# Decoding float64 weight words on ScalarE, VectorE and GpSimd: sign by the slope of a parametric Relu, low bits by a pass of ScalarE, one joining pass on VectorE

## The chip, the cores and the metric

One core of a Trainium2 chip. The metric is the device time of one execution in microseconds (us). The kernel before took 958.51 us, the median of 3 runs (957.35 to 958.92).

## What is computed

```python
def reference(q, k, v, w_in, w_out, a, b):        # q, k, v: (8, 8, 576, 64)
    scores = q @ k.T / sqrt(64)                   # causal window of 64 positions
    x = softmax(scores within the window) @ v     # then (B, H, S, D) -> (4608, 512)
    h = x @ w_in                                  # (512, 2048)
    P = a[0] + a[1]*h + a[2]*h**2 + a[3]*h**3
    Q = 1 + abs(b[0])*abs(h) + abs(b[1])*h**2
    return (P / (Q + 1e-6)) @ w_out               # (2048, 512)
```

The two weight matrices arrive as float64. They are handed to the kernel as pairs of 32-bit words, low word first, and the kernel itself makes float32 of them.

## The kernel before

**Tiling.** The 4608 tokens are nine chunks of 512 (`c`). The attention of a chunk is four units `(c, hp)`, one for each pair of heads: scores on TensorE, exponentials on ScalarE, a normalisation on GpSimd (L589), transposes on TensorE, a copy `pT` to SBUF, the product with v (`ps_x`, L608). From `ps_x` come `xh`, a rounded copy, and `xl`, the rest (L613, L617). The feed-forward part goes in steps: step `s` takes one chunk and one 128-wide slice `i` of the 2048 hidden channels. It makes `h` by twelve products of `wi_h`, `wi_l` with `xh`, `xl` (L688), passes `h` through a gate of five ScalarE passes, six VectorE passes and one GpSimd product `u1` (L694 to L733), and adds twelve products of the gate with `wo_h`, `wo_l` into four accumulators (L771). The steps run chunk 0 with slices 0 to 7, then chunk 1 with slices 0 to 15, then chunk 0 with slices 8 to 15, then chunks 2 to 8 with all slices. So the first eight steps, of chunk 0, are steps 0 to 7, and step 8 is the first of chunk 1.

**The decode** (`plan_decode`) makes 32 weight tiles, sixteen of `w_in` and sixteen of `w_out`; tile `n = 2i + z` holds slice `i`. Per tile: a load of 512 KB by SP; `scale` on ScalarE (L393) multiplies the high word, read as float32, by 2^-111 into `w_c`, or into a bank of PSUM from slice 8 on; `sign` on GpSimd (L397) multiplies the high word by zero in place, which leaves its sign bit; `put_sign` on VectorE (L401) shifts `w_c` left by 3 and ors the sign in; `put_low` on VectorE (L406) ors in the top three bits of the low word; `high` on ScalarE (L417) rounds to `wi_h` or `wo_h`; `rest` on VectorE (L420) gives `wi_l` or `wo_l`.

**The order** is made before anything runs by `Plan`. Every operation is added with an engine, a cost, a rank, what it follows and which buffers (`Slot`) it uses. `Plan.order` walks these in a model of time and hands the operations out by their planned start, so every engine's queue is in that order and is never reordered on the chip. Ranks are shifted by tables of numbers (`TILE_AT`, `UNIT_AT`, `GATE_AT`, `OUT_AT`, `FETCH_AT`), and `LI`, `LO` say how many steps before its first use a tile's decode is ranked. `PT_DVE` and `XH_DVE` name the units whose `pT` copy and `xh` copy VectorE makes; ScalarE makes the others.

Of the kernel before, what the change touches and what calls it, by code (L numbers as in the profile page):

```python
# [45 lines left out]
class Plan:  # L46
# [25 lines left out]
    def order(self):  # L72
# [22 lines left out]
        while len(done) < len(self.ops):  # L95
            best = None
            for e in ENGINES:
                able = []
                for op in ready[e]:
                    if e == "SP" and op.rank > now + self.ahead:  # L100
                        continue
                    if any(not slots[s.pool] for s in op.takes):
                        continue
                    t = max([free[e], op.ready + op.late] + [min(slots[s.pool]) for s in op.takes])
                    if op.port:
                        t = max(t, port["POOL" if e == "DVE" else "DVE"])
                    if e == "SP":
                        t = max(t, bus - 2.5)
                    able.append((t, op))
                if not able:  # L110
                    continue
                t0 = min(t for t, _ in able)
                t, op = min(((t, op) for t, op in able if t <= t0 + 0.02), key=lambda x: (x[1].rank, x[0], x[1].n))
                if best is None or t < best[0]:
                    best = t, op
            t, op = best
# [64 lines left out]
def swa_rational_ffn(ctx: ExitStack, tc: tile.TileContext, qT, kT, v, w_in, w_out, a, b, out):  # L181
    nc = tc.nc
# [19 lines left out]
    tmp = ctx.enter_context(tc.tile_pool(name="tmp", bufs=2))  # L202
    gp = ctx.enter_context(tc.tile_pool(name="gp", bufs=3))
# [92 lines left out]
    EC = 2  # L296
    PF = 3
    HA = H
    LI, LO = (4, 1.5), (2, 1.5)
    C0R, AH = -12.0, (2, 2, 3.0)  # L300
    TILE_AT = {12: -0.5, 17: -0.5, 18: -2, 20: -1.5, 4: 0.25}
    FETCH_AT = {(0, 2): -0.5, (2, 0): -2, 12: 1}
    UNIT_AT = {(0, 1): 2, (1, 0): -1.5, (2, 0): -0.5}
    GATE_AT = {13: 1, 18: 1.25, 22: -1, 31: 0.25, 33: -0.75, 34: -2, 36: -1}
    OUT_AT = {25: -2, 5: -3}
# [70 lines left out]
    def plan_decode(i, src, his, los, rank, z):  # L376
        in_psum = i >= PSC
        n = 2 * i + z
        plan.shift = TILE_AT.get(n, 0.0)
        home = HOMES[n % len(HOMES)] if n < FROM else "w_st"  # L380
        st, sc = Slot(home), Slot(f"b{z}" if in_psum else "kt" if n % 3 == 2 else "w_c")
        d = {}

        def load():
# [433 lines left out]
    for p, (c, i0, i1) in enumerate(phases):  # L818
# [57 lines left out]
```

## Time and profile before

| what | value |
|---|---|
| median of 3 runs | 958.51 us |
| the profiled execution, its own time | 959.0 us |
| its span, first to last instruction | 957.0 us |
| mean granted TensorE clock over the span | 0.993 |
| busy share of TensorE (PE), VectorE (DVE), ScalarE (ACT), GpSimd (POOL) | 98%, 83%, 70%, 35% |

The page gives shares over the whole span. A share of 98% for one engine says which engine is the limit on the whole, and not where its few idle microseconds lie; for that the page's 40 slices, tables of busy time by stretch and the timeline of one engine are read. On all of these an operation's duration includes some overlap with the next one on its engine: the time that it takes from its queue is the distance from its start to the next start.

### The profile page before, as it was taken

Reading aid. Unit: us, or ns where it says so; the run is one execution under the profiler, and the core shown is the slowest. Engines: PE = TensorE matmul, PEld = TensorE weight load, DVE = VectorE, ACT = ScalarE, POOL = GpSimd, SP = SyncE. Lnnn points to the kernel's source line nnn. Section 1 sums busy time; section 2 is a strip of 40 time slices with the busy share of each in tenths; the row PEclk is TensorE's granted clock in tenths of the full one; section 3 lists DMA queues with packets and bytes.
Section 4 is the critical chain, followed back from the end, with each engine's and each line's share of the span. In section 5 each row is a group of like instructions: output and inputs, shape, how many; then the busy total and the mean of one; then the engine's idle time right before and its main releaser. Section 6 shows DMA issues by size and latency. Waiting matters only on the chain.

```text
span 957.0 us, 16313 instructions
## 1 busy us (share of the span) xinstructions
PE 934.6 (98%) x6068; PEld 752.0 (79%) x6068; DVE 791.6 (83%) x1198; ACT 669.8 (70%) x1477; POOL 330.7 (35%) x227
## 2 busy tenths in 40 slices
PE   7798999999999999999999999999999999999998
PEld 4576778778888888888888888888888888888886
DVE  5999999999797977887787787887879778777775
ACT  6788777778767577676776677667676676756564
POOL 4756355533323233233323233233132332322221
PEclk9799999999999999999999999999999999999999
DMA  8831323122421112101211121111211121001001
GB/s 301 280 108 45 121 99 113 66 91 85 137 98 44 44 44 71 58 2 54 76 44 44 43 76 54 45 48 48 92 46 46 46 78 35 1 1 45 0 1 45
DMA packets 39103, 66.47 MB, mean 69 GB/s; under 512 B 5616, under 2 KB 22256, under 8 KB 39024
## 3 DMA queue, kind: packets, MB, share of 16 engines
q1 hardware_dynamic: 39024, 65.43, 20.9%
q8 instruction: 48, 0.79, 0.3%
q14 instruction: 31, 0.25, 0.1%
HBM read 54.92 MB, written 10.49 MB: 68 GB/s over the span
## 4 chain that ended last, share of the span: by engine, by line
PE 82%; DVE 11%; issue 2%; DMA 2%; ACT 1%; POOL 0%; SPq 0%; ACTq 0%; DVEq 0%; POOLq 0%
PE o L771 37%; PE h L688 36%; PE ps_x L608 3%; PE banks L527 3%; PE banks L594 2%; DMA w_st<-w_in 2%; DVE gh L720 2%; DVE num L703 1%; DVE gl L733 1%; DVE num L728 1%; DVE u L724 1%; DVE num L706 1%; DVE bank L401 1%; DVE w_c L401 1%; ACT sm L577 1%
## 5 line engine op out<-in xcount | busy, mean ns | idle before, releaser
L710 POOL TENSOR_TENSOR u<-u,ah 128x512 f32<-128x512 f32 x144 | 203.1, 1410 | 422.9 <-ACT u L700 294.9
L688 PE MATMUL h<-xl,wi_h 128*128 128x512 f32 x576 | 230.5, 400 | 4.8 <-DVE num L706 3.2
L771 PE MATMUL o<-wo_h,gl 128*128 128x512 f32 x576 | 231.9, 403 | 0.3 <-ACT ob L783 0.2
L688 PE MATMUL h<-xh,wi_l 128*128 128x512 f32 x576 | 227.8, 396 | 0.0
L688 PE MATMUL h<-xh,wi_h 128*128 128x512 f32 x576 | 227.5, 395 | 0.0
L771 PE MATMUL o<-wo_h,gh 128*128 128x512 f32 x576 | 226.7, 393 | 0.0
L771 PE MATMUL o<-wo_l,gh 128*128 128x512 f32 x576 | 225.8, 392 | 0.0
L713 ACT ACTIVATE ah<-u 128x512 f32<-128x512 f32 x144 | 91.0, 633 | 114.8 <-POOL u L710 114.7
L720 DVE SCALAR_TENSOR_TENSOR gh<-num,a_sb,ah 128x512 fp32r<-128x512 f32 x144 | 111.3, 773 | 49.9 <-ACT ah L716 48.5
L694 ACT ACTIVATE ah<-h 128x512 f32<-128x512 f32 x144 | 85.9, 597 | 81.9 <-PE h L688 56.8
L703 DVE TENSOR_TENSOR num<-num,h 128x512 f32<-128x512 f32 x144 | 98.3, 683 | 45.5 <-ACT num L697 45.3
L688 PEld LDWEIGHTS h<-xl,wi_h 128*128 128x128 f32 x576 | 108.5, 188 | 34.0 <-DVE num L706 4.8
L771 PEld LDWEIGHTS o<-wo_h,gl 128*128 128x128 f32 x576 | 108.2, 188 | 26.9 <-issue 3.1
L688 PEld LDWEIGHTS h<-xh,wi_l 128*128 128x128 f32 x576 | 108.5, 188 | 26.1
L688 PEld LDWEIGHTS h<-xh,wi_h 128*128 128x128 f32 x576 | 108.7, 189 | 24.8
L771 PEld LDWEIGHTS o<-wo_h,gh 128*128 128x128 f32 x576 | 108.1, 188 | 25.2
L771 PEld LDWEIGHTS o<-wo_l,gh 128*128 128x128 f32 x576 | 108.3, 188 | 22.6
L589 POOL TENSOR_TENSOR sm<-sm,rs 128x1024 f32<-128x1024 f32 x36 | 69.8, 1940 | 159.4 <-ACT ah L694 88.1
L728 DVE SCALAR_TENSOR_TENSOR num<-num,a_sb,u 128x512 f32<-128x512 f32 x144 | 115.9, 806 | 2.3
L700 ACT ACTIVATE u<-ah,b_sb 128x512 f32<-128x512 f32 x144 | 117.3, 815 | 0.0
L724 DVE SCALAR_TENSOR_TENSOR u<-u,gh 128x512 f32<-128x512 f32 x144 | 106.2, 738 | 7.1
L697 ACT ACTIVATE num<-h,a_sb 128x512 f32<-128x512 f32 x144 | 111.9, 777 | 0.0
(80 smaller groups left out, 1095.3 us busy)
## 6 DMA issues: line engine op xcount, KB each, us to landing
out<-ob SPq DMA_DIRECT2D x35, 256.0 KB, 2.0
w_st<-w_in SPq DMA_DIRECT2D x16, 512.0 KB, 5.2
w_st<-w_out SPq DMA_DIRECT2D x16, 512.0 KB, 4.1
vt<-v SPq DMA_DIRECT2D x8, 448.0 KB, 5.7
vt<-v SPq DMA_DIRECT2D x8, 384.0 KB, 3.3
vt<-v SPq DMA_DIRECT2D x8, 320.0 KB, 3.9
q<-qT SPq DMA_DIRECT2D x8, 256.0 KB, 4.8
kt<-kT SPq DMA_DIRECT2D x8, 256.0 KB, 4.3
```

The source lines that it names most:

```text
L589: nc.gpsimd.tensor_tensor(out=sm, in0=sm, in1=u["rs"].unsqueeze(2).broadcast_to([P, NR, P]), op=ALU.mult)
L688: nc.tensor.matmul(h, w[i][:, cc, :], x[c, cc], start=n == 0, stop=n == 3 * NCC - 1)
L694: nc.scalar.activation(d["ah"], d["h"], AF.Abs)
L697: nc.scalar.activation(d["num"], d["h"], AF.Identity, scale=a_sb[:, 3:4], bias=a_sb[:, 2:3])
L700: nc.scalar.activation(d["u"], d["ah"], AF.Identity, scale=b_sb[:, 1:2], bias=b_sb[:, 0:1])
L703: nc.vector.tensor_tensor(out=d["num"], in0=d["num"], in1=d["h"], op=ALU.mult)
L710: nc.gpsimd.tensor_tensor(out=d["u"], in0=d["u"], in1=d["ah"], op=ALU.mult)
L713: nc.scalar.activation(d["ah"], d["u"], AF.Ln, bias=QADD)
L720: nc.vector.scalar_tensor_tensor(out=d["gh"], in0=d["num"], scalar=a_sb[:, 0:1], in1=d["ah"], op0=ALU.add, op1=ALU.mult)
L724: nc.vector.scalar_tensor_tensor(out=d["u"], in0=d["u"], scalar=QADD, in1=d["gh"].bitcast(F32), op0=ALU.add, op1=ALU.mult)
L728: nc.vector.scalar_tensor_tensor(out=d["num"], in0=d["num"], scalar=a_sb[:, 0:1], in1=d["u"], op0=ALU.add, op1=ALU.subtract)
L771: nc.tensor.matmul(acc[t], g[:, ts], w[i], start=first and n == 0, stop=last and n == 2)
```

## The change

The high word's upper 16 bits are first clamped from below on GpSimd (`guard`), so that no negative word has too small an exponent. `scale` becomes a parametric Relu whose slope for negative input is -2^32: a negative word comes out positive with another exponent, so that the shift by 3 brings up a one in the sign's place. `low` is a new pass of ScalarE that reads the upper half of the low word as a 16-bit integer and writes its top three bits, as a number, over the low word. `join_words` on VectorE shifts `w_c` and ors the three bits in, in one pass. `guard` has to come before `scale`; before the change `scale` came first and `sign` followed. The numbers of the planner's tables are new, the planner takes operations within 0.1 us of each other by rank (0.02 before), and VectorE makes one more pair of `pT` copies and one more `xh` copy.

```diff
-                t, op = min(((t, op) for t, op in able if t <= t0 + 0.02), key=lambda x: (x[1].rank, x[0], x[1].n))
+                t, op = min(((t, op) for t, op in able if t <= t0 + 0.1), key=lambda x: (x[1].rank, x[0], x[1].n))
...
-    LI, LO = (4, 1.5), (2, 1.5)
-    C0R, AH = -12.0, (2, 2, 3.0)
-    TILE_AT = {12: -0.5, 17: -0.5, 18: -2, 20: -1.5, 4: 0.25}
...
+    LI, LO = (1.5, 1.5), (2.0, -2)
+    C0R, AH = -12, (1, 3, 2.9)
+    TILE_AT = {12: -0.5, 17: -0.5, 18: -2, 28: 1, 4: 0.25}
...
-    UN, GT, F2R, OUTR, N1, SG, LD = 0.3, 0.02, 0.5, -0.5, 0.0, 0, 2.0
+    UN, GT, F2R, OUTR, N1, SG, LD = 0.2, 0.02, 0.25, 0, 0.6, 0.0, 3
     KEEP = 4
-    PT_DVE = ((0, 0), (0, 1))
-    XH_DVE = ((0, 0), (0, 1))
+    LOW_ACT = range(32)
+    PT_DVE = ((0, 0), (0, 1), (0, 2))
+    XH_DVE = ((0, 1), (0, 2), (0, 3))
...
+        def half(k, dt):
+            return d["w"].bitcast(dt).rearrange("p n (w h) -> p n w h", h=2)[:, :, k, 1]
+
+        def guard():
+            top = half(1, I16)
+            nc.gpsimd.tensor_scalar(out=top, in0=top, scalar1=float(LEAST), scalar2=None, op0=ALU.max)
+
         def scale():
             c = d["c"] = banks[z].bitcast(U32) if in_psum else words(n)
-            nc.scalar.activation(c.bitcast(F32), d["w"].bitcast(F32)[:, :, 1], AF.Copy, scale=2.0 ** -111)
-
-        def sign():
-            highf = d["w"].bitcast(F32)[:, :, 1]
-            nc.gpsimd.tensor_scalar(out=highf, in0=highf, scalar1=0.0, scalar2=None, op0=ALU.mult)
-
-        def put_sign():
+            nc.scalar.activation(c.bitcast(F32), d["w"].bitcast(F32)[:, :, 1], AF.Prelu, scale=2.0 ** -111, alpha=-2.0 ** 32)
+
+        def low():
+            t, u = d["w"][:, :, 0], half(0, U16)
+            if n in LOW_ACT:
+                nc.scalar.activation(t, u, AF.Identity, scale=2.0 ** -13, bias=FLOOR)
+            else:
+                nc.gpsimd.tensor_scalar(out=t, in0=u, scalar1=2.0 ** -13, scalar2=FLOOR, op0=ALU.mult, op1=ALU.add)
+
+        def join_words():
             c = d["c"]
-            nc.vector.scalar_tensor_tensor(out=c, in0=c, scalar=3, in1=d["w"][:, :, 1], op0=ALU.logical_shift_left,
-                                           op1=ALU.bitwise_or)
-
-        def put_low():
-            c = d["c"]
-            nc.vector.scalar_tensor_tensor(out=c, in0=d["w"][:, :, 0], scalar=29, in1=c, op0=ALU.logical_shift_right,
+            nc.vector.scalar_tensor_tensor(out=c, in0=c, scalar=3, in1=d["w"][:, :, 0], op0=ALU.logical_shift_left,
                                            op1=ALU.bitwise_or)
...
-        o = plan.add("ACT", 0.66, rank, scale, [o], [st, sc])
-        o = plan.add("POOL", 1.57, rank - SG, sign, [o], [st], 0.55)
-        o = plan.add("DVE", 0.688, rank, put_sign, [o], [st, sc], 0.0 if in_psum else 0.688)
-        o = plan.add("DVE", 0.688, rank, put_low, [o], [st, sc], 0.0 if in_psum else 0.688)
+        by_act = n in LOW_ACT
+        g = plan.add("POOL", 1.57, rank - SG, guard, [o], [st], 0.55)
+        t = plan.add("ACT" if by_act else "POOL", 0.66 if by_act else 1.57, rank - SG, low, [o], [st], 0.0 if by_act else 0.55)
+        o = plan.add("ACT", 0.66, rank, scale, [g], [st, sc])
+        o = plan.add("DVE", 0.688, rank, join_words, [o, t], [st, sc], 0.0 if in_psum else 0.688)
```

What the new numbers do is seen in the order of the instructions. On SP, the last load of v of chunk 0 and the four loads of q and k of unit (1, 0) stood behind the first load of `w_in` and now stand ahead of it. On ScalarE, `low` of this first tile and the `xh` copy of unit (0, 0) now stand ahead of the exponentials of unit (0, 3), where `scale` of the tile stood before.

GpSimd, from the first normalisations (units of chunk 0, L589 before and L600 now) to the products u1 of the first steps; `w_st` is a staged weight tile, its pass `sign` before (L397) and `guard` now (L401). Before, and then now:

```order
L589 TENSOR_TENSOR sm<-sm,rs 128x1024 x2
L397 TENSOR_SCALAR w_st<-w_st 128x512
L589 TENSOR_TENSOR sm<-sm,rs 128x1024 x2
L397 TENSOR_SCALAR w_st<-w_st 128x512 x7
L589 TENSOR_TENSOR sm<-sm,rs 128x1024
L710 TENSOR_TENSOR u<-u,ah 128x512
```

```order
L600 TENSOR_TENSOR sm<-sm,rs 128x1024 x2
L401 TENSOR_SCALAR w_st<-w_st 128x512
L600 TENSOR_TENSOR sm<-sm,rs 128x1024
L401 TENSOR_SCALAR w_st<-w_st 128x512
L600 TENSOR_TENSOR sm<-sm,rs 128x1024
L401 TENSOR_SCALAR w_st<-w_st 128x512 x10
L600 TENSOR_TENSOR sm<-sm,rs 128x1024
L721 TENSOR_TENSOR u<-u,ah 128x512
```

Eight weight tiles went ahead of the normalisation of unit (1, 0); now it is twelve, ten of them in a row.

ScalarE, the last passes ahead of the exponentials of unit (1, 0) (L577 before, L588 now) and the first `abs` of a gate behind them (L694, L705). `scale` is L393 before and L405 now, `high` is L417 and L427, `low` is L410. Before, and then now:

```order
L393 ACTIVATE w_c<-w_st 128x512
L613 CAST xh_0_577<-ps_x 128x512
L417 ACTIVATE wi_h_149<-w_c 128x512
L393 ACTIVATE w_c<-w_st 128x512
L417 ACTIVATE wo_h_135<-w_c 128x512
L577 ACTIVATE sm,sums<-bank_168,nmx 128x128 x4
L577 ACTIVATE sm,sums<-bank_169,nmx 128x128 x4
L694 ACTIVATE ah<-h 128x512
```

```order
L405 ACTIVATE w_c<-w_st 128x512 x2
L410 ACTIVATE w_st<-w_st 128x512
L405 ACTIVATE w_c<-w_st 128x512
L410 ACTIVATE w_st<-w_st 128x512
L427 ACTIVATE wo_h_139<-w_c 128x512
L410 ACTIVATE w_st<-w_st 128x512
L588 ACTIVATE sm,sums<-bank_168,nmx 128x128 x4
L588 ACTIVATE sm,sums<-bank_169,nmx 128x128 x4
L705 ACTIVATE ah<-h 128x512
```

Before and now the eighth `scale` of the program is the last one ahead of these exponentials; now three `low` passes stand among the last six instructions, and ten of them in all stand ahead.

TensorE at the product with v of the last unit of chunk 1 (`vt_874` before, `vt_902` now; L608, L619). `wi_h_161` is slice 7, which is used by step 7; `wo_h_147` and `wo_h_151` are slices 3 and 4. Before, and then now:

```order
L594 MATMUL bank_168<-ident_r,sm 128x128 x4
L594 MATMUL bank_169<-ident_r,sm 128x128 x4
L771 MATMUL o_833<-wo_h_147,gl 128x512
L771 MATMUL o_833<-wo_l_148,gh 128x512
L771 MATMUL o_833<-wo_h_147,gh 128x512
L608 MATMUL ps_x<-pT,vt_874 64x64 x16
L771 MATMUL o_783<-wo_h_151,gl 128x512
L771 MATMUL o_783<-wo_l_152,gh 128x512
```

```order
L699 MATMUL h<-xl_0_519,wi_h_161 128x512
L699 MATMUL h<-xh_0_511,wi_h_161 128x512
L699 MATMUL h<-xh_0_511,wi_l_162 128x512
L699 MATMUL h<-xl_0_586,wi_h_161 128x512
L699 MATMUL h<-xh_0_579,wi_h_161 128x512
L699 MATMUL h<-xh_0_579,wi_l_162 128x512
L619 MATMUL ps_x<-pT,vt_902 64x64 x16
L782 MATMUL o_772<-wo_h_151,gl 128x512
L782 MATMUL o_772<-wo_l_152,gh 128x512
L782 MATMUL o_772<-wo_h_151,gh 128x512
```

The twelve products of step 7 came behind this `ps_x` and now come ahead of it, as do the first three L771 products of slice 4. Between it and the next `h` stand twelve L771 products before and twenty-one now.

## Rows read from the trace of the kernel before

**Rows 1.** The page, parts 1 and 2: the span; busy us, share of the span and instructions of each engine; of the 40 equal slices (23.9 us each) the busy tenths of PE and DVE and the granted TensorE clock in tenths.
```profile
span 957.0 us, 16313 instructions
PE 934.6 (98%) x6068; PEld 752.0 (79%) x6068; DVE 791.6 (83%) x1198; ACT 669.8 (70%) x1477; POOL 330.7 (35%) x227
...
PE   7798999999999999999999999999999999999998
...
DVE  5999999999797977887787787887879778777775
...
PEclk9799999999999999999999999999999999999999
```

**Rows 2.** Busy time by stretch: the stretch and its length, then busy us and instructions of PE, PEld, DVE, ACT, POOL in this order, the mean granted clock, the DMA share, GB/s.
```profile
0.00:95.00 95.00, 76.79 (x743) 58.33 (x744) 82.06 (x140) 72.55 (x214) 57.45 (x47) 0.93 0.55 185
95.00:953.00 858.00, 857.42 (x5326) 693.70 (x5325) 709.09 (x1058) 596.50 (x1262) 273.22 (x180) 1.00 0.17 56
...
40.30:88.00 47.70, 43.21 (x355) 33.71 (x353) 45.36 (x74) 43.52 (x121) 28.62 (x19) 0.96 0.35 109
...
48.60:52.00 3.40, 3.40 (x9) 2.65 (x8) 3.36 (x6) 3.40 (x18) 1.28 (x1) 0.50 0.00 0
...
94.30:190.00 95.70, 95.12 (x405) 75.61 (x406) 95.34 (x152) 71.51 (x119) 46.75 (x31) 1.00 0.29 100
```

**Rows 3.** Timeline of PE (start us, duration us, engine, line, operation, output<-inputs, count, and in brackets the idle time before it with its releaser): the waits between 25 and 95 us that the text uses.
```profile
27.06 0.33 PE L608 MATMUL ps_x<-pT,vt 128*64 128x64 f32 x2 [2.89 <-ACT pT L602]
...
47.81 0.50 PE L688 MATMUL h<-xl,wi_h 128*128 128x512 f32 x1 [2.23 <-DVE num L706]
...
59.25 1.15 PE L608 MATMUL ps_x<-pT,vt 128*64 128x64 f32 x32 [0.89 <-DVE num L706]
...
62.60 1.15 PE L608 MATMUL ps_x<-pT,vt 128*64 128x64 f32 x32 [0.61 <-DVE xl L617]
...
79.22 0.49 PE L688 MATMUL h<-xl,wi_h 128*128 128x512 f32 x1 [0.75 <-DVE num L706]
...
88.58 1.15 PE L608 MATMUL ps_x<-pT,vt 128*64 128x64 f32 x32 [0.55 <-ACT bank L393]
...
94.29 0.50 PE L688 MATMUL h<-xl,wi_h 128*128 128x512 f32 x1 [1.61 <-DVE xl L617]
```

**Rows 4.** From the chain of work that ended last, in order of time (start us, us, what, count): one block of twelve products at the full clock.
```profile
102.91 2.80 PE h L688 x12
```

**Rows 5.** Groups of instructions by line and form over the whole run (busy us, mean ns of one | idle time before them): the decode passes that the change touches, and the copy of pT that VectorE makes.
```profile
L393 ACT ACTIVATE w_c<-w_st 128x512 f32<-128x512 f32 x16 | 10.9, 687 | 4.6 <-DVE wi_l L420 4.1 <-DMA w_st<-w_in 0.5
...
L393 ACT ACTIVATE bank<-w_st 128x512 f32<-128x512 f32 x16 | 10.2, 639 | 3.1 <-DVE wi_l L420 1.3 <-DMA w_st<-w_out 1.1 <-DVE wo_l L420 0.7
...
L397 POOL TENSOR_SCALAR w_st<-w_st 128x512 f32<-128x512 f32 x32 | 55.7, 1747 | 31.5 <-DVE gl L733 9.4 <-ACT w_c L393 6.5 <-DVE gh L720 4.9
...
L406 DVE SCALAR_TENSOR_TENSOR w_c<-w_st,w_c 128x512 uint32<-128x512 uint32 x16 | 11.1, 701 | 0.0
...
L406 DVE SCALAR_TENSOR_TENSOR bank<-w_st,bank 128x512 uint32<-128x512 uint32 x16 | 10.9, 683 | 0.0
...
L602 DVE COPY pT<-bank 128x512 f32<-128x512 f32 x4 | 2.5, 671 | 0.0
```

**Rows 6.** Timeline of ACT, columns as in group 3: the second and third scaling pass, the first of the sixteen instructions of the exponentials of unit (1, 0), what follows them, and the last pair of pT copies of chunk 1.
```profile
22.11 0.70 ACT L393 ACTIVATE w_c<-w_st 128x512 f32<-128x512 f32 x1
...
23.34 0.69 ACT L393 ACTIVATE w_c<-w_st 128x512 f32<-128x512 f32 x1 [0.54 <-DMA w_st<-w_in]
...
40.33 0.37 ACT L577 ACTIVATE sm<-bank,nmx 128x128 f32<-128x128 f32 x1 [0.85 <-DVE nmx L566]
...
43.09 0.64 ACT L694 ACTIVATE ah<-h 128x512 f32<-128x512 f32 x1
43.57 0.68 ACT L417 ACTIVATE wi_h<-w_c 128x512 fp32r<-128x512 f32 x1
44.09 0.83 ACT L697 ACTIVATE num<-h,a_sb 128x512 f32<-128x512 f32 x1
44.75 0.87 ACT L700 ACTIVATE u<-ah,b_sb 128x512 f32<-128x512 f32 x1
45.46 0.65 ACT L694 ACTIVATE ah<-h 128x512 f32<-128x512 f32 x1
45.93 0.72 ACT L393 ACTIVATE w_c<-w_st 128x512 f32<-128x512 f32 x1
46.49 0.84 ACT L697 ACTIVATE num<-h,a_sb 128x512 f32<-128x512 f32 x1
...
86.92 1.08 ACT L602 COPY pT<-bank 128x512 f32<-128x512 f32 x2
```

**Rows 7.** Who ACT waited for between 40.3 and 88 us: engine, line, us in total, times, longest.
```profile
ACT sm L577 <- DVE nmx L566: 2.8, 3, 1.4
ACT w_c L393 <- DVE wi_l L420: 1.3, 2, 0.8
```

**Rows 8.** POOL: the group of the sign pass between 20 and 46 us, then from its timeline the normalisation of unit (1, 0) and the product u1 of the first step.
```profile
L397 POOL TENSOR_SCALAR w_st<-w_st 128x512 f32<-128x512 f32 x8 | 13.7, 1724 | 4.5 <-ACT w_c L393 3.8 <-POOL w_st L397 0.7
...
43.85 1.90 POOL L589 TENSOR_TENSOR sm<-sm,rs 128x1024 f32<-128x1024 f32 x1 [3.21 <-ACT ah L694]
45.70 1.27 POOL L710 TENSOR_TENSOR u<-u,ah 128x512 f32<-128x512 f32 x1
```

More of the change, by code (lines that the diff above doesn't have):

```diff
@@ L12 @@
 U32 = mybir.dt.uint32
+U16 = mybir.dt.uint16
+I16 = mybir.dt.int16
 AF = mybir.ActivationFunctionType
@@ L25 @@
 QADD = 1.0 + 1e-6
+LEAST = 888 * 16 - (1 << 15)
+FLOOR = 2.0 ** -14 - 0.5
 class Slot:
@@ L298, in swa_rational_ffn @@
     HA = H
-    LI, LO = (4, 1.5), (2, 1.5)
-    C0R, AH = -12.0, (2, 2, 3.0)
-    TILE_AT = {12: -0.5, 17: -0.5, 18: -2, 20: -1.5, 4: 0.25}
[L302 to L305, printed above, removed]
-    UN, GT, F2R, OUTR, N1, SG, LD = 0.3, 0.02, 0.5, -0.5, 0.0, 0, 2.0
+    LI, LO = (1.5, 1.5), (2.0, -2)
+    C0R, AH = -12, (1, 3, 2.9)
+    TILE_AT = {12: -0.5, 17: -0.5, 18: -2, 28: 1, 4: 0.25}
+    FETCH_AT = {(0, 2): -0.5, (2, 0): -2, 12: 1, 13: 0.25}
+    UNIT_AT = {(0, 1): 2, (1, 0): -1.5, (1, 1): -1, (2, 0): -0.5}
+    GATE_AT = {13: 1, 18: 1.25, 22: -1, 29: 4, 31: 0.25, 33: -0.75, 34: -1.5, 36: -1, 6: -1}
+    OUT_AT = {0: 0.25, 17: -2, 25: 1, 5: -3}
+    UN, GT, F2R, OUTR, N1, SG, LD = 0.2, 0.02, 0.25, 0, 0.6, 0.0, 3
     KEEP = 4
-    PT_DVE = ((0, 0), (0, 1))
-    XH_DVE = ((0, 0), (0, 1))
+    LOW_ACT = range(32)
+    PT_DVE = ((0, 0), (0, 1), (0, 2))
+    XH_DVE = ((0, 1), (0, 2), (0, 3))
     LENT = ((0, 1),)
@@ L353, in swa_rational_ffn @@
     plan = Plan({"w_st": 3, "w_c": WC, "b0": 1, "b1": 1, "kt": 1, "e0": 4, "e1": 2, "sme": 2, "pTe": 2, "sm": 2, "vt": 1, "pT": 1, "h": 2,
-                 "tmp": 2, "gp": 3, "o0": 1, "o1": 1, "o2": 1, "o3": 1}, 5.0)
+                 "tmp": 2, "gp": 3, "o0": 1, "o1": 1, "o2": 1, "o3": 1}, 4.0)
     ready_in, ready_out = {}, {}
```

## The prediction, made before the changed kernel was run

> **What bounds the kernel now.** I read the page first: PE is busy 98% of the span, so only its idle and slow time can be gained [rows 1]. The slices place that time: PE's digits are 9 but for the first four slices, and the granted clock falls in the second. The table by stretch closes it in: in the first 95 us PE is busy 76.8, so 18.2 us are idle; in the 858 us behind that it is busy 857.4 [rows 2]. Nothing that this change does behind 95 us can bring more than 0.6 us, and the decode of the weights fills the stretch ahead of it.
>
> The timeline of PE gives the waits there [rows 3]. Two kinds matter. At 47.81, 59.25, 79.22 (2.23, 0.89, 0.75 us) PE waits for VectorE's num2, which frees a bank of h, and at 62.60 and 94.29 (0.61 and 1.61 us) for VectorE's xl. At 27.06 and 88.58 (2.89 and 0.55 us) it waits behind ScalarE. VectorE is busy 45.4 of the 47.7 us from 40.3 to 88, ScalarE 43.5 [rows 2]: two nearly full engines in strict order. The wait at 47.81 is followed by a stretch at the lower level of the clock, 1.2 GHz: from 48.6 to 52.0 the granted clock is 0.50, and PE gets through 9 instructions in 3.4 us [rows 2], where twelve products in a block at the full clock take 2.80 us [rows 4], 0.233 each. That stretch costs 3.4 - 9 x 0.233 = 1.3 us.
>
> **The change, part by part.** *VectorE* loses put_low: 32 passes, 22.0 us [rows 5]. It gains one pair of pT copies and an xh copy, 3 x 0.67 = 2.0 us by the row of pT. *ScalarE* gains 32 low passes; the nearest rows are its own scale passes, 0.69 us into SBUF and 0.64 into PSUM [rows 5], so 20 to 22 us, and loses those three copies. Its place in the queue is the distance of two starts: scale to num0 is 0.56 us (45.93 to 46.49) [rows 6]. I price low at that; it cannot be much below, and and u0, the same function with a scale and a bias, takes 0.71 (44.75 to 45.46) [rows 6]. Prelu for Copy is priced at nothing: the same elements on the same engine. *GpSimd* swaps sign for guard, one for one. A 16-bit pass is not in the trace. The nearest row is sign, 1.72 us between 20 and 46 us [rows 8]; I take that, with 1.3 (u1, 512 elements of two inputs, [rows 8]) and 2.6 (half as much again) as bounds.
>
> So the work does not shrink, it moves from the fuller engine to the second. What counts is when the last ps_x of chunk 1 (88.58 before) can start, since that is where both orders meet and where the waits end.
>
> *Ahead of it* the new order puts twelve more h products (2.80 us, [rows 4]) and three more L771 (0.7). *Behind it* stand 21 instead of 12 L771 products: 1.1 + 21 x 0.233 = 6.0 us of cover for the chain from there to xl, which took 94.29 - 88.58 = 5.7; so the wait of 1.61 [rows 3] goes. If V is the new start of that ps_x, the gain is 2.8 + 0.7 + 1.6 - (V - 88.58) = 5.1 - (V - 88.58).
>
> *V* comes out of a walk through GpSimd and ScalarE.
> - Five DMAs now stand ahead of the first w_in load. Scale passes started at 22.11 and at 23.34, the latter as its load landed [rows 6]; the first load now lands about where the second did less one such distance, some 20.7 us. ScalarE has low of this tile ahead of the exponentials of unit (0, 3).
> - GpSimd: guard 20.7 to 22.4, normalise (0, 2) 1.9 us [rows 8] to 24.3, guard to 26.0, normalise (0, 3) to 27.9, then ten guards in a row: the sixth, the eighth of all, ends at 27.9 + 6 x 1.72 = 38.2, the tenth at 45.1.
> - The eighth scale waits for the eighth guard; behind it come low, high, low: 38.2 + 3 x 0.56 + 0.52 = 40.4, the start of the exponentials of unit (1, 0). It was 40.33 [rows 6].
> - From there to the last pT copies of chunk 1 (86.92, done at 88.0 [rows 6]) ScalarE was busy 43.5 us. The new order has in that piece six low, one scale less, one high more and abs, num0 and u0 of one more step: 6 x 0.56 - 0.56 + 0.52 + 0.48 + 0.66 + 0.71 = 5.2 [rows 6]. So 48.7.
> - Waits of ScalarE in this piece: 4.2 us before (47.7 - 43.5, [rows 2]), nearly all on VectorE's maxima (2.8) and on rest, which frees a buffer (1.3) [rows 7]. VectorE loses nine passes here, 5 us, and I take these waits as gone. A new one takes their place: normalise (1, 0) stands behind the tenth guard and ends at 47.0, and u1 of step 0 behind it (1.3, [rows 8]) at 48.3. ScalarE has its logarithm 4.1 us behind the exponentials' end: 40.4 + 2.8 + 4.1 = 47.2. It waits 1.1, and all its queue with it.
> - V = 40.4 + 48.7 + 1.1 + 0.5 = 90.7.
>
> The gain is 5.1 - 2.1 = **3.0 us**. PE itself could be there earlier: from 38 to 88.58 it has 5.0 us of waits [rows 3] and 1.3 of slow clock [rows 2], so 44 us of work and 3.5 more, which ends by 86.
>
> Behind 95 us ScalarE gets sixteen low passes, up to 11 us, on 71.5 busy of 95.7 between 94.3 and 190 [rows 2]: 82. VectorE falls from 95.3 to 84. PE did not wait beside a VectorE that was full there, so I cost it at nothing; if the cover failed, the last decodes would come late, which the 11 us bound.
>
> The sum against the profiled execution: 959.0 - 3.0 = 956.0; that run is 0.5 above the median of 958.51, so the forecast for the median is **955.5 us**.
>
> **Rivals.**
> 1. *ScalarE is not the bound.* Guards pack tighter, ScalarE's walk shortens, and all six waits from 47.81 on vanish: 2.23 + 0.89 + 0.61 + 0.75 + 0.55 + 1.61 = 6.6 us [rows 3]. For: PE's work allows it. Against: 48.7 us of ScalarE in the walk. 952.
> 2. *ScalarE takes over VectorE's role.* Its 4.2 us of waits stay, with or without the new 1.1: V = 93.8 to 94.9, a change of 0.0 to +1.2: 958.5 to 959.7, no change that a measurement (some 0.2%, 1.9 us) can tell. For: it is now the fuller one of two engines in strict order, and scale hangs behind GpSimd. Against: what it waited for was VectorE.
> 3. *The guards are dearer than sign.* Twelve of them stand ahead of normalise (1, 0), and u1, the logarithm and the exponentials of unit (1, 1) queue behind it: each 0.1 us on a guard is 1.2 us. At 1.97 us the gain is gone; from 2.13 the kernel is slower by 0.2%; at 2.22 it is 961.5. For: a 16-bit read and write in place is untried, and sign with its one input already takes more than u1 with two (1.72 against 1.27, [rows 8]). Against: the same number of elements at the same step in bytes. The Trainium skill (GPSIMD Engine Reference, Performance pitfalls for Q7 kernels) says that reading at a step of over 8 bytes costs about 2.9 instead of 1.9 cycles an element, a 16-bit step of more than 4 among them. The guard's step is 4, so by that rule this rival falls away. The trace agrees on no figure of it (1.9 cycles would be 0.81 us for 512 elements, an estimate from that page, and sign at 8 bytes takes 1.72), so I leave the rival its chance.
>
> That the change is not carried out as described would not move the time: the order shows one low, one guard and one joining pass for a tile, and one table load as before.
>
> **How the numbers follow.** The forecast (ScalarE's walk with 1.1 us of wait) 0.45, around 955.5; rival 1 0.15; rival 2 0.20; rival 3 0.20. The walk's own error, some 1.5 us at the landing of the load and as much in the waits, puts a ninth of the forecast into "same". Faster by over 0.2%: 0.40 + 0.15 = 0.55; within: 0.20 + 0.05 = 0.25; slower: 0.20. The range takes in rival 1, rival 2 and rival 3 up to 2.2 us a guard: 951.5 to 961.5.
>
> **What would show it.** Guards of 1.6 to 1.8 us, low passes near 0.65; the exponentials of unit (1, 0) starting at 39 to 42; the logarithm of step 0 waiting for u1; the last ps_x of chunk 1 at 89 to 92, with no wait of PE for xl behind it; VectorE below 93% and ScalarE above 93% between 40 and 90; idle time of PE in the first 95 us some 3 us less, and less than 1 us behind. It would be wrong if the exponentials start later than 43 or if PE waits for weights behind 95 us; and wrong in its reason if PE gains ahead of 40 us.

## The result, and the profile after

The changed kernel takes **966.54 us** (median of 6 runs, 965.89 to 967.58) where the kernel before takes 958.75 beside it: ratio 1.0084, 95% interval 1.0071 to 1.0097. It is slower by 7.8 us, where the prediction had it 3.0 faster and its range ended at 961.5. The profiled execution took 967.58 us; its span is 965.8, 8.8 more than before.

The page, parts 1 and 2, with the columns of [rows 1]:
```profile
span 965.8 us, 16288 instructions
...
PE 937.5 (97%) x6068; PEld 753.7 (78%) x6068; DVE 784.4 (81%) x1169; ACT 684.2 (71%) x1506; POOL 341.1 (35%) x227
...
PE   6869999999999999999999999999999999999998
...
POOL 4994377433223322222223222222222222222221
PEclk9799999999999999999999999999999999999999
```
PE's third slice fell from 9 to 6, and GpSimd has two nines (24 to 72 us). Over the whole span GpSimd still shows 35%, as before: the share of the span hides it.

Busy time by stretch, columns as in [rows 2]:
```profile
0.00:95.00 95.00, 73.29 (x697) 55.04 (x698) 72.83 (x124) 74.77 (x221) 65.11 (x46) 0.93 0.55 185
...
95.00:953.00 858.00, 854.99 (x5335) 691.58 (x5334) 706.24 (x1038) 606.02 (x1281) 274.72 (x181) 1.00 0.17 56
...
40.00:90.00 50.00, 41.34 (x330) 31.35 (x323) 43.63 (x69) 44.80 (x123) 35.18 (x18) 0.99 0.37 116
...
120.00:160.00 40.00, 37.95 (x158) 30.41 (x157) 36.27 (x55) 34.28 (x59) 30.65 (x17) 0.96 0.43 149
```
VectorE is rid of its work as intended (72.8 us in the first 95, 82.1 before [rows 2]), and ScalarE has little more (74.8 against 72.6). Still PE is idle for 21.7 us there, 18.2 before, and for 3.0 us behind, 0.6 before. Neither VectorE nor ScalarE is full between 40 and 90 us: 87% and 90%. Both wait. The last row is of the second stretch of decodes, and is used further down.

The groups of the touched passes (busy us, mean ns | idle before), as in [rows 5]:
```profile
L401 POOL TENSOR_SCALAR w_st<-w_st 128x512 int16<-128x512 int16 x32 | 75.9, 2453 | 5.5 <-DMA w_st<-w_in 3.9 <-DMA w_st<-w_out 1.6
...
L410 ACT ACTIVATE w_st<-w_st 128x512 uint32<-128x512 uint16 x32 | 22.6, 724 | 3.2 <-DMA w_st<-w_in 3.2
...
L405 ACT ACTIVATE w_c<-w_st 128x512 f32<-128x512 f32 x16 | 11.1, 692 | 6.0 <-POOL w_st L401 5.1 <-DVE wi_l L430 0.5 <-DVE wo_l L430 0.3
```
L401 is the guard, L410 low, L405 scale. low costs what was forecast, Prelu costs what Copy cost (692 against 687 ns). **The guard takes 2.45 us**, where sign took 1.75 [rows 5], and ScalarE's scaling waits 5.1 us for it. The timeline of GpSimd, columns as in [rows 8]:
```profile
20.44 2.23 POOL L401 TENSOR_SCALAR w_st<-w_st 128x512 int16<-128x512 int16 x1 [2.78 <-DMA w_st<-w_in]
...
28.28 22.66 POOL L401 TENSOR_SCALAR w_st<-w_st 128x512 int16<-128x512 int16 x10
50.75 1.91 POOL L600 TENSOR_TENSOR sm<-sm,rs 128x1024 f32<-128x1024 f32 x1
52.61 1.29 POOL L721 TENSOR_TENSOR u<-u,ah 128x512 f32<-128x512 f32 x1
```
The first guard starts where the walk had it (20.4, forecast 20.7). The ten in a row stand 22.47 / 10 = 2.25 us apart, so normalise (1, 0) starts at 50.75 instead of 45.1, and u1 of step 0 ends at 53.9 instead of 48.3. ScalarE's timeline shows who hangs on it:
```profile
42.21 0.66 ACT L405 ACTIVATE w_c<-w_st 128x512 f32<-128x512 f32 x1 [1.03 <-POOL w_st L401]
...
44.42 0.35 ACT L588 ACTIVATE sm<-bank,nmx 128x128 f32<-128x128 f32 x1
...
53.93 0.63 ACT L724 ACTIVATE ah<-u 128x512 f32<-128x512 f32 x1 [2.55 <-POOL u L721]
```
The scaling waits for a guard, so the exponentials of unit (1, 0) start at 44.42 (40.33 before [rows 6]). The logarithm of step 0 waits 2.55 us for u1, and with it all that stands behind it on ScalarE. PE's timeline, columns as in [rows 3], has the price:
```profile
35.43 2.45 PE L619 MATMUL ps_x<-pT,vt 128*64 128x64 f32 x32 [3.95 <-ACT pT L613]
...
50.54 0.50 PE L699 MATMUL h<-xl,wi_h 128*128 128x512 f32 x1 [1.65 <-DVE num L717]
...
55.17 0.50 PE L699 MATMUL h<-xl,wi_h 128*128 128x512 f32 x1 [1.57 <-DVE num L717]
...
60.27 0.50 PE L782 MATMUL o<-wo_h,gl 128*128 128x512 f32 x1 [0.98 <-DVE gl L744]
...
64.70 1.09 PE L605 MATMUL bank<-ident_r,sm 128*128 128x128 f32 x8 [1.40 <-POOL sm L600]
...
98.16 1.15 PE L619 MATMUL ps_x<-pT,vt 128*64 128x64 f32 x32
...
142.83 0.50 PE L699 MATMUL h<-xl,wi_h 128*128 128x512 f32 x1 [2.05 <-DVE num L717]
...
178.75 0.50 PE L699 MATMUL h<-xl,wi_h 128*128 128x512 f32 x1 [0.94 <-DVE num L717]
```
VectorE is named in most of these waits, but it had been waiting itself (it is 87% busy from 40 to 90 us). The last ps_x of chunk 1, the V of the prediction, starts at 98.16 instead of 90.7. The wait for xl behind it is gone, as forecast. The two waits at 142.83 and 178.75 lie in the second stretch of decodes, where GpSimd alternates between guards and u1:
```profile
126.49 6.94 POOL L401 TENSOR_SCALAR w_st<-w_st 128x512 int16<-128x512 int16 x3 [1.12 <-DMA w_st<-w_in]
133.25 1.43 POOL L721 TENSOR_TENSOR u<-u,ah 128x512 f32<-128x512 f32 x1
...
146.44 6.47 POOL L401 TENSOR_SCALAR w_st<-w_st 128x512 int16<-128x512 int16 x3
152.72 1.32 POOL L721 TENSOR_TENSOR u<-u,ah 128x512 f32<-128x512 f32 x1
```
What hangs on the u1 of 133.25 is seen on ScalarE, whose logarithm waits for it, and then on VectorE, whose joining pass waits for the scaling that stands behind that logarithm:
```profile
134.72 0.63 ACT L724 ACTIVATE ah<-u 128x512 f32<-128x512 f32 x1 [2.22 <-POOL u L721]
```
```profile
135.91 0.70 DVE L416 SCALAR_TENSOR_TENSOR bank<-bank,w_st 128x512 uint32<-128x512 uint32 x1 [2.37 <-ACT bank L405]
```
From there VectorE works without a pause, and the num for which PE waits until 142.83 is made only at 142.03.

Behind the first of PE's two waits its clock falls: 9 products from 143.63 to 147.28 take 3.65 us, at the full clock 9 x 0.233 = 2.1, so 1.55 us more; the stretch from there on, columns as in [rows 2]:
```profile
142.80:146.40 3.60, 3.57 (x10) 2.86 (x11) 3.60 (x6) 3.60 (x8) 3.06 (x2) 0.63 0.39 132
```
The granted clock is 0.63 there, mostly the lower level, 1.2 GHz.

**The account.** The prediction's identity, gain = 5.1 - (V - 88.58), gives 5.1 - 9.6 = -4.5 us. Behind the meeting point PE idles 3.0 - 0.6 = 2.4 us more, and 1.55 go to the clock: 8.5 of the 8.8 us by which the span of the profiled execution grew. (That execution is 1.0 us above the median of the changed kernel, so the fall of the clock need not be in every one.)

### The profile page after: what moved, and what is told of

Read it like the earlier page. It is cut to its first block, busy times and chain, and to the rows that moved or that the text cites. A ratio compares the mean times of both kernels' runs of the same rounds, so it can differ in the third digit from the quotient of the medians.

```text
span 965.8 us, 16288 instructions
## 1 busy us (share of the span) xinstructions
PE 937.5 (97%) x6068; PEld 753.7 (78%) x6068; DVE 784.4 (81%) x1169; ACT 684.2 (71%) x1506; POOL 341.1 (35%) x227
## 3 DMA queue, kind: packets, MB, share of 16 engines
q1 hardware_dynamic: 39024, 65.43, 20.7%
## 4 chain that ended last, share of the span: by engine, by line
PE 81%; DVE 5%; POOL 4%; DMA 4%; issue 3%; ACT 3%; SPq 0%; POOLq 0%; DVEq 0%; ACTq 0%
PE o L782 37%; PE h L699 36%; PE ps_x L619 3%; POOL w_st L401 3%; PE banks L538 3%; PE banks L605 2%; DMA w_st<-w_in 2%; DVE num L739 1%; DMA b_raw<-b 1%; DVE u L735 1%; POOL u L721 1%; DVE num L714 1%; DVE num L717 1%; ACT sm L588 1%; DMA q<-qT 1%
## 5 line engine op out<-in xcount | busy, mean ns | idle before, releaser
L721 POOL TENSOR_TENSOR u<-u,ah 128x512 f32<-128x512 f32 x144 | 195.4, 1358 | 486.6 <-ACT u L711 365.3
L731 DVE SCALAR_TENSOR_TENSOR gh<-num,a_sb,ah 128x512 fp32r<-128x512 f32 x144 | 126.5, 879 | 76.7 <-ACT ah L727 76.5
L705 ACT ACTIVATE ah<-h 128x512 f32<-128x512 f32 x144 | 85.9, 597 | 121.7 <-PE h L699 92.2
L739 DVE SCALAR_TENSOR_TENSOR num<-num,a_sb,u 128x512 f32<-128x512 f32 x144 | 113.2, 786 | 3.0
L600 POOL TENSOR_TENSOR sm<-sm,rs 128x1024 f32<-128x1024 f32 x36 | 69.1, 1920 | 120.1 <-ACT ah L724 49.8
L735 DVE SCALAR_TENSOR_TENSOR u<-u,gh 128x512 f32<-128x512 f32 x144 | 103.5, 719 | 8.3 <-DVE gh L731 0.5
```

The costliest lines, as they stand in the source:

```text
L600: nc.gpsimd.tensor_tensor(out=sm, in0=sm, in1=u["rs"].unsqueeze(2).broadcast_to([P, NR, P]), op=ALU.mult)
L705: nc.scalar.activation(d["ah"], d["h"], AF.Abs)
L721: nc.gpsimd.tensor_tensor(out=d["u"], in0=d["u"], in1=d["ah"], op=ALU.mult)
L731: nc.vector.scalar_tensor_tensor(out=d["gh"], in0=d["num"], scalar=a_sb[:, 0:1], in1=d["ah"], op0=ALU.add, op1=ALU.mult)
L735: nc.vector.scalar_tensor_tensor(out=d["u"], in0=d["u"], scalar=QADD, in1=d["gh"].bitcast(F32), op0=ALU.add, op1=ALU.mult)
L739: nc.vector.scalar_tensor_tensor(out=d["num"], in0=d["num"], scalar=a_sb[:, 0:1], in1=d["u"], op0=ALU.add, op1=ALU.subtract)
```

## The experiments

Theory 1: the price of the guard is the whole loss, since it stands ahead of the scaling, of normalise and of u1 in GpSimd's strict order. Theory 2: that the scaling waits for a GpSimd pass at all is the loss. Theory 3: the new order, or ScalarE's 32 more passes, is the loss. All but the eighth were timed beside the kernel before, whose median was between 958.4 and 958.8 us in each group of runs.

| kernel | us | ratio to before, 95% interval | V, us |
|---|---|---|---|
| changed kernel | 966.54 | 1.0084 (1.0071 to 1.0097) | 98.16 |
| 1 guard as fp32 product | 956.32 | 0.9974 (0.9965 to 0.9984) | 91.64 |
| 2 no guard | 953.46 | 0.9949 (0.9932 to 0.9966) | 88.47 |
| 3 order planned for 2.25 us | 968.28 | 1.0101 (1.0086 to 1.0116) | 96.09 |
| 4 guard on consecutive halves | 958.96 | 1.0003 (0.9994 to 1.0013) | 92.17 |
| 5 before, with a 16-bit pass | 966.42 | 1.0080 (1.0063 to 1.0097) | 91.48 |
| 6 before, new numbers | 983.17 | 1.0255 (1.0240 to 1.0271) | 93.11 |
| 7 no guard, numbers of before | 960.57 | 1.0021 (1.0012 to 1.0030) | 95.95 |
| 9 fp32 for the first 17 | 960.00 | 1.0009 (1.0000 to 1.0018) | 91.67 |
| 10 fp32 for the last 15 | 963.00 | 1.0045 (1.0030 to 1.0060) | 97.32 |
| 11 no guard, scale twice | 967.19 | 1.0088 (1.0072 to 1.0105) | 96.30 |
| 12 scaling's product on GpSimd | 956.48 | 0.9978 (0.9969 to 0.9987) | 91.47 |

(V is the start of the last ps_x of chunk 1. With other planning numbers, 3 and 5 to 7, another set of products stands around it, so there it is not to be compared with the rest; kernel 5 has the order of the kernel before, whose V is 88.58.)

**1. The guard in the form of sign.**
```
-            top = half(1, I16)
-            nc.gpsimd.tensor_scalar(out=top, in0=top, scalar1=float(LEAST), scalar2=None, op0=ALU.max)
+            highf = d["w"].bitcast(F32)[:, :, 1]
+            nc.gpsimd.tensor_scalar(out=highf, in0=highf, scalar1=1.0, scalar2=None, op0=ALU.mult)
```


> The changed kernel with its guard (GpSimd, 16-bit maximum, 2.45 us in its trace) replaced by a multiplication by 1.0 of the same 128x512 high words as fp32, the form of the pass that the kernel before has (1.75 us there); every queue keeps its order. It leaves out the clamp of very small words. Theory 1 (the price of the guard is the loss): 954 to 958 us, exps of unit (1, 0) at 40 to 42 us instead of 44.4, the waits at 142.8 and 178.8 us gone. Theory 2 (that ScalarE's scaling waits for a GpSimd pass at all is the loss, whatever its price): 964 us or more. Theory 3 (the new order of the queues, or ScalarE's 32 more passes, are the loss): 964 us or more as well.

956.32 us: theory 1, and 0.8 us from the forecast of 955.5. The group of L401, three rows of GpSimd's timeline, one of ScalarE's and one of PE's:
```profile
L401 POOL TENSOR_SCALAR w_st<-w_st 128x512 f32<-128x512 f32 x32 | 54.3, 1715 | 7.2 <-DMA w_st<-w_in 4.6 <-DVE u L735 2.5
```
```profile
26.96 14.55 POOL L401 TENSOR_SCALAR w_st<-w_st 128x512 f32<-128x512 f32 x9
43.38 1.57 POOL L401 TENSOR_SCALAR w_st<-w_st 128x512 f32<-128x512 f32 x1 [1.87 <-DMA w_st<-w_in]
44.90 1.89 POOL L600 TENSOR_TENSOR sm<-sm,rs 128x1024 f32<-128x1024 f32 x1
```
```profile
41.11 0.37 ACT L588 ACTIVATE sm<-bank,nmx 128x128 f32<-128x128 f32 x1 [0.27 <-DVE nmx L577]
```
```profile
91.64 1.15 PE L619 MATMUL ps_x<-pT,vt 128*64 128x64 f32 x32
```
With guards of 1.72 us in the mean the walk's times come out within 1 us: normalise (1, 0) at 44.90 (45.1), exponentials at 41.11 (40.4), V at 91.64 (90.7). The first of these is luck in part: nine guards of the row take 14.55 / 9 = 1.62 us each, less than the walk had, and the tenth waits 1.87 us for a load that the walk left out. The identity then gives 5.1 - 3.06 = 2.0 us; 2.3 were measured. One wait of PE behind 95 us stays, 1.13 us at 168.2 (0.6 us idle there before), which the identity leaves out.

**2. No guard.**
```
         def guard():
-            top = half(1, I16)
-            nc.gpsimd.tensor_scalar(out=top, in0=top, scalar1=float(LEAST), scalar2=None, op0=ALU.max)
+            pass
```


> The changed kernel without its guard: ScalarE's scaling waits for the words alone; every queue keeps its order. It leaves out the clamp of very small words. Theory 1: 951 to 957 us, at or below the kernel with the fp32 pass. Theory 2: 951 to 957 us too, but at least 5 us below the kernel with the fp32 pass. Theory 3: 962 us or more, with ScalarE over 95% busy between 40 and 90 us.

953.46 us, 2.9 below kernel 1: theory 2 asked for 5 at least. V is 88.47, and the identity gives 5.1 + 0.1 = 5.2 us; 5.2 were measured. ScalarE is now full between 40 and 90 us (second of the busy numbers from the right):
```profile
40.00:90.00 50.00, 46.76 (x402) 36.61 (x401) 44.72 (x76) 49.66 (x130) 17.78 (x11) 1.00 0.33 103
```

**3. The order planned for the real price.**
```
-        g = plan.add("POOL", 1.57, rank - SG, guard, [o], [st], 0.55)
+        g = plan.add("POOL", 2.25, rank - SG, guard, [o], [st], 0.55)
```


> The changed kernel, where the planner is told 2.25 us for the guard instead of 1.57, and so writes another order of the queues; the operations are the same. Theory 1: the guards still take 32 x 2.25 us of GpSimd's time, but the order can put normalise and u1 further ahead: 959 to 965 us. If the order made for the wrong price was the larger part of the loss (theory 3): 957 us or less. If the order hardly matters: 965 to 968 us.

968.28 us, 1.7 slower than the changed kernel and just above the highest of the three bands: a miss of the band that I gave theory 1, and it speaks against the order as the larger part. A planner that knows the price does not save what the pass costs; whether other tables would is open.

**4. The same 16-bit pass without its step.**
```
-            top = half(1, I16)
+            top = d["w"].bitcast(I16).rearrange("p n four -> p (n four)")[:, 0:512]
```


> The changed kernel with the guard's 16-bit maximum on the first 512 consecutive 16-bit halves of the tile, instead of every fourth one: same count, same type, no step. It so works on other halves than the scaling needs. If the 16-bit type sets the price: the guard takes 2.2 to 2.5 us again, and the time is 965 to 968 us. If the step of 8 bytes sets it: 1.9 us or less, and by theory 1 the time is 951 to 958 us.

```profile
L401 POOL TENSOR_SCALAR w_st<-w_st 128x512 int16<-128x512 int16 x32 | 50.7, 1594 | 10.9 <-ACT w_st L410 4.8 <-DMA w_st<-w_in 3.1 <-DVE u L735 2.6
...
L410 ACT ACTIVATE w_st<-w_st 128x512 uint32<-128x512 uint16 x32 | 21.1, 678 | 5.4 <-POOL w_st L401 5.3
```
1.59 us: the 16-bit type alone is not dear. The time, 958.96, is a little above the band. This pass also touches halves that low works on: low waits 5.3 us for it, and it waits 4.8 us for low, which the changed kernel has not. That this is the reason for the 2.6 us above kernel 1 is likely and not shown.

**5. The kernel before, with a pass as dear.**
```
-            highf = d["w"].bitcast(F32)[:, :, 1]
-            nc.gpsimd.tensor_scalar(out=highf, in0=highf, scalar1=0.0, scalar2=None, op0=ALU.mult)
+            top = d["w"].bitcast(mybir.dt.int16).rearrange("p n (w h) -> p n w h", h=2)[:, :, 1, 1]
+            nc.gpsimd.tensor_scalar(out=top, in0=top, scalar1=0.0, scalar2=None, op0=ALU.mult)
```


> The kernel before, whose GpSimd pass (x 0 of the high words as fp32, 1.75 us) becomes a 16-bit pass (x 0) of every fourth half of the same tile; the orders are those of before. The weights so lose their signs and keep some low bits. There the pass is not ahead of ScalarE's scaling, but of VectorE's joining. If what counts is GpSimd's time alone (theory 1): the pass takes 2.2 to 2.5 us, and the kernel loses 6 to 12 us, so 964 to 970 us. If the loss comes from the place ahead of ScalarE's scaling (theory 2): 958 to 961 us.

```profile
L397 POOL TENSOR_SCALAR w_st<-w_st 128x512 int16<-128x512 int16 x32 | 77.2, 2446 | 29.7 <-DVE gl L733 9.4 <-DVE gh L720 4.8 <-ACT w_c L393 4.6
```
966.42 us, with 2.45 us a pass. The old kernel loses 8.0 us by a pass of the same price, though there it is ahead of VectorE's joining and not of the scaling. Theory 2 falls. The pass here is a product and the guard a maximum, so the operation does not make the price either.

**6 and 7. Numbers and operations apart.** Kernel 6 is the kernel before with the changed tables, tie window, lists and limit on how far the loads may be planned ahead; kernel 7 is kernel 2 with those of before.
```
-    LI, LO = (4, 1.5), (2, 1.5)
+    LI, LO = (1.5, 1.5), (2.0, -2)
...
-    PT_DVE = ((0, 0), (0, 1))
+    PT_DVE = ((0, 0), (0, 1), (0, 2))
...
```


> The kernel before, its operations unchanged, with the changed kernel's planning numbers (the tables, the 0.1 us tie window, the pT and xh lists). If the numbers are worth nothing by themselves: 957 to 962 us. If the 5.2 us that the kernel without the guard gains are mostly the order: 953 to 956 us. If the numbers only suit the new operations: 962 us or more.

> The changed operations without the guard, with the planning numbers of the kernel before. It leaves out the clamp of very small words. If the 5.2 us that the kernel without the guard gains come from VectorE's 32 passes less: 953 to 956 us. If they need the new numbers: 957 us or more.

983.17 and 960.57 us. The new numbers cost the old operations 24.7 us, and the new operations without them lose 2.1 against before, and 7.1 against kernel 2. Both fall into the last band of their expectations: the numbers suit only the new operations, and the operations need the new numbers. Moving 32 passes from VectorE to ScalarE brings nothing in the old order. The gain comes when the order is made for them, which is what the 5.1 of the identity (15 more products ahead of V, nine more behind it) stands for.

**8. The price by itself.** Twenty passes of 128x512 behind the last work of the changed kernel, with nothing beside them (one execution; only the rows are used).
```
+        for name, k, dt, step in (("pa", 3, I16, 4), ("pb", 1, I16, 2), ("pc", 0, I16, 1), ("pd", 1, F32, 2), ("pe", 0, F32, 1)):
...
+            v = w.rearrange("p n two -> p (n two)").bitcast(dt).rearrange("p (n s) -> p n s", s=step)[:, 0:512, k]
+            for _ in range(4):
+                if dt == I16:
+                    nc.gpsimd.tensor_scalar(out=v, in0=v, scalar1=float(LEAST), scalar2=None, op0=ALU.max)
+                else:
+                    nc.gpsimd.tensor_scalar(out=v, in0=v, scalar1=1.0, scalar2=None, op0=ALU.mult)
```


> The changed kernel with 20 more GpSimd passes of 128x512 behind its last one, nothing beside them: four each of the 16-bit maximum on every fourth half (pa), every second half (pb), consecutive halves (pc), of the fp32 product on every second word (pd) and on consecutive words (pe). If the step of 8 bytes sets the price: pa 2.2 to 2.3 us, pc and pe 1.6 us or less, pd near pa. If it is the type with the step: pa 2.2 to 2.3, pd 1.5 to 1.6 as in the trace of the kernel with the fp32 pass, pb between pa and pc.

```profile
L861 POOL TENSOR_SCALAR pa<-pa 128x512 int16<-128x512 int16 x4 | 8.8, 2210 | 10.2 <-DVE pa L857 9.9
L861 POOL TENSOR_SCALAR pb<-pb 128x512 int16<-128x512 int16 x4 | 6.5, 1624 | 0.2
L863 POOL TENSOR_SCALAR pd<-pd 128x512 f32<-128x512 f32 x4 | 6.1, 1532 | 0.3
L863 POOL TENSOR_SCALAR pe<-pe 128x512 f32<-128x512 f32 x4 | 5.9, 1487 | 0.2
L861 POOL TENSOR_SCALAR pc<-pc 128x512 int16<-128x512 int16 x4 | 5.9, 1483 | 0.2
```
Neither the type nor the step in bytes alone sets the price: 16-bit halves consecutive 1.48, every second 1.62, every fourth 2.21; fp32 words at the same 8 bytes 1.53. The step counted in elements would fit all five rows as well (1.48 and 1.49 at one, 1.62 and 1.53 at two, 2.21 at four); fp32 words at a step of four, which would tell the two apart, were not run. Nor do the runs show whether the reading or the writing at that step is dear.

**9 and 10. Where the loss lies.** The guard is the fp32 product for the first 17 tiles (9), or, with `> 17` in the condition, for the 15 behind them (10).
```
+            guards.append(n)
+            if len(guards) <= 17:
+                highf = d["w"].bitcast(F32)[:, :, 1]
+                nc.gpsimd.tensor_scalar(out=highf, in0=highf, scalar1=1.0, scalar2=None, op0=ALU.mult)
+                return
```


> The changed kernel with the fp32 product by 1.0 as guard for the first 17 tiles in GpSimd's order (those of the first 95 us) and the 16-bit maximum for the other 15. It leaves out the clamp for the 17. By PE's idle time between the kernels with either guard (21.6 against 15.0 us in the first 100 us, 3.0 against 1.1 us from 120 to 200), the early guards carry some 7 of the 10.2 us: 957.5 to 960 us. If the waits at 142.8 and 178.8 us follow from the early delay and not from the later guards: 955.5 to 957.5 us. If the late guards carry most: 961 us or more.

> The other half: 16-bit maximum for the first 17 tiles, fp32 product for the 15 behind them, whose clamp it leaves out. Early guards carry some 7 us: 963 to 965.5 us. Late guards carry most: 961 us or less. The two parts add up if its gain and that of the other half make 10 us together.

960.00 and 963.00 us. The dear guards behind 95 us cost 960.00 - 956.32 = 3.7 us, those ahead 963.00 - 956.32 = 6.7; together 10.4, where both at once cost 966.54 - 956.32 = 10.2. So the two stretches lose independently. Both times lie on the edge of the bands that gave the early guards the larger part. Who PE waited for between 95 and 200 us (us, times, longest), kernel 9 and then kernel 10:
```profile
PE h L705 <- DVE num L723: 4.1, 4, 2.1
```
```profile
PE h L705 <- DVE num L723: 1.1, 1, 1.1
```
The longest wait of kernel 9 is as long as the one at 142.83 of the changed kernel, but the clock did not fall behind it (PE's timeline, then busy time by stretch):
```profile
136.10 0.50 PE L705 MATMUL h<-xl,wi_h 128*128 128x512 f32 x1 [2.11 <-DVE num L723]
```
```profile
120.00:160.00 40.00, 37.72 (x163) 30.08 (x162) 37.13 (x56) 34.11 (x58) 33.00 (x17) 1.00 0.37 125
```

**11. ScalarE's share.** Kernel 2 with the scaling pass done twice.
```
             nc.scalar.activation(c.bitcast(F32), d["w"].bitcast(F32)[:, :, 1], AF.Prelu, scale=2.0 ** -111, alpha=-2.0 ** 32)
+            nc.scalar.activation(c.bitcast(F32), d["w"].bitcast(F32)[:, :, 1], AF.Prelu, scale=2.0 ** -111, alpha=-2.0 ** 32)
```


> The changed kernel without the guard, with ScalarE's scaling done twice (the same pass again, some 0.66 us x 32), every queue otherwise in the same order. It leaves out the clamp of very small words. If ScalarE bounds the first 95 us, as the prediction has it: about 0.6 us for each of the some 17 tiles there, 6 to 12 us more, 959 to 966 us, and exps of unit (1, 1) later by as much. If ScalarE has slack there: 953 to 956 us.

967.19 us, 13.7 more, above the band. V is 7.8 us later; behind it PE waits 4.4 us between 95 and 200 us (0.7 idle in kernel 2), 3.7 more; the other 2.2 I can't place. Busy time in the stretch from 20 to 95 us, kernel 2 and then kernel 11:
```profile
20.00:95.00 75.00, 64.98 (x579) 51.25 (x580) 66.36 (x112) 71.63 (x184) 22.32 (x14) 0.95 0.47 164
...
20.00:95.00 75.00, 61.81 (x518) 48.64 (x519) 59.78 (x100) 74.11 (x186) 20.97 (x13) 0.89 0.44 153
```
ScalarE (the fourth busy number) has 71.6 of 75 us in kernel 2 and 74.1 with the added passes. Some 17 x 0.56 = 9.5 us were added there, and V moved by most of that: without a dear guard ScalarE bounds this stretch, as the forecast had it, and behind 95 us it is not free either.

**12. The scaling's product on GpSimd.**
```
-            top = half(1, I16)
-            nc.gpsimd.tensor_scalar(out=top, in0=top, scalar1=float(LEAST), scalar2=None, op0=ALU.max)
+            highf = d["w"].bitcast(F32)[:, :, 1]
+            nc.gpsimd.tensor_scalar(out=highf, in0=highf, scalar1=2.0 ** -111, scalar2=None, op0=ALU.mult)
...
-            nc.scalar.activation(c.bitcast(F32), d["w"].bitcast(F32)[:, :, 1], AF.Prelu, scale=2.0 ** -111, alpha=-2.0 ** 32)
+            nc.scalar.activation(c.bitcast(F32), d["w"].bitcast(F32)[:, :, 1], AF.Prelu, scale=1.0, alpha=-2.0 ** 32)
```


> The changed kernel, whose GpSimd pass is an fp32 product by 2^-111 of the high words (the scaling's factor, in the form of the pass of the kernel before), with ScalarE's pass then keeping only the slope, at scale 1. Same price as the kernel with the product by 1.0: 955.5 to 957 us, faster than before by 0.15 to 0.3%. If the pass that makes tiny numbers costs more on GpSimd or ScalarE: 957 us or more.

956.48 us, 2.3 below before, as expected. GpSimd's product takes over the scaling's factor, at 1.70 us a pass. Words too small for fp32 after that factor come to the slope as GpSimd leaves them; what it leaves of a negative one, which the 16-bit maximum is there for, was not tried.

## Why the prediction was wrong

**The step that failed is the guard's price**, taken from the row of sign at 1.72 us. It is 2.25 us from start to start and 2.45 as a row. The bounds that I gave, 1.3 and 2.6, held it; the value taken inside them did not. Sign was the nearest row by count and by step in bytes, and the two passes differ in what those leave out: elements of 16 bits, every fourth. Kernel 8 shows just that difference (2.21 against 1.53 us). Kernel 1 shows that with it removed the forecast holds to 0.8 us: the price of the guard carries 966.54 - 956.32 = 10.2 of the 11.0 us by which the forecast was off.

- *Rival 3 is what happened*, with its mechanism and its place. It said 12 us for each us on a guard; at 2.25 it gives (2.25 - 1.97) x 12 = 3.4 us slower, and 7.8 came. Most of what is missing is the stretch behind 95 us: 3.7 us by kernel 9.
- *The stretch behind 95 us, costed at nothing*, failed for that reason. I looked at VectorE and ScalarE there and not at GpSimd, whose 15 guards stand between the u1 products: it is busy 30.7 us of 40 from 120 to 160. Its u1 gates the logarithm, and with it the whole step. Kernel 11 adds that ScalarE is near full there too.
- *The 5.1 us of the new order and the identity* held in kernels 1 and 2 (2.0 and 5.2 computed, 2.3 and 5.2 measured).
- *The walk* held up to the guards: first load 20.4 (20.7), exponentials in kernel 1 at 41.1 (40.4), V 91.6 (90.7). low cost 0.72 us as a row and 0.56 from start to start, Prelu what Copy cost. Some of it held by luck: in kernel 1 guards of 1.62 us and a wait of 1.87 us for a load add up to the forecast's row of ten, and the logarithm of step 0 starts at 48.07 (48.3) without the 1.1 us of wait for u1 that the walk gave it. And one distance of 1.23 us ahead of the scaling at 22.11 is 20.9, not the 20.7 that the walk began with.
- *Rival 1* (ScalarE has slack) is answered by kernels 2 and 11: no. *Rival 2* (ScalarE takes VectorE's place, at no gain) did not come: kernel 1 is 0.26% faster.
- *What would show it*: of the two marks named as fatal the first came, exponentials later than 43 (44.42). The second came in another form: PE waited 3.0 us behind 95 us, but for num, which frees a bank of h, and not for weights. ScalarE was forecast above 93% between 40 and 90 us and was at 90%, as it waited.

The Trainium skill (GPSIMD Engine Reference, Performance pitfalls for Q7 kernels) has the dear reads begin at a step of over 8 bytes, for 16-bit elements above 4. Here the rise is there at exactly 8 bytes for 16-bit elements (2.21 against 1.48 us for consecutive ones) and not for fp32 (1.53 against 1.49). The page differs from this measurement of a built-in pass that reads and writes at that step, and the measurement decides. I had kept the rival's chance at 0.20 against that rule, and should have kept more: 2 in 10 of the chance lay on the one pass whose type no row had, while the other new passes had near rows that held.

## What to carry to other kernels

Price an untried pass by type and step together, and where only a neighbour's row exists, let the end of the range follow the dear bound through the whole queue behind it. An engine at 35% of the span can still set the time: look at its busy share in the stretch, and at what stands behind its pass in order. When work moves between engines, the order has to be made anew for it (7.1 us here), and the gain and its price show only together.

## What the hardware showed that I had not expected

- GpSimd, 128x512 in place, nothing beside it: 16-bit halves at a step of one, two and four halves take 1.48, 1.62 and 2.21 us, fp32 words at a step of one and two 1.49 and 1.53. In the kernel, beside the other engines, the one at a step of four halves took 2.24 to 2.81 us and the fp32 one at a step of two words 1.72 in the mean. No run has fp32 at a step of four words.
- One wait of PE of 2.05 us, at 142.83, was followed by a lower granted clock for 3.65 us, which cost another 1.55 us. A wait of 2.11 us at 136.10 of kernel 9 was not (1.00 granted), so the length of the wait does not settle it.
